# Convolution and two MLPs on one core: a new order of the first steps, and the low part of two chunks taken by one subtraction

## The chip, the cores and the metric

One core of a Trainium2 chip runs the whole program as one launch. The metric is device time in microseconds (us), the median of several executions of the same program.

## The reference

Each of 4 sequences of 4096 tokens with 192 channels goes through a causal convolution of 7 taps whose weights are a softmax per head (8 heads of 24 channels). The result, 16384 tokens by 192, goes through two MLPs with 2048 hidden units:

```python
w = softmax(weight)                                    # 8 heads x 7 taps
x = einsum('hk,bskhg->bshg', w, windows_of(x_padded))  # causal convolution
h = x @ w_in1;  x = (h - tanh(h)) @ w_out1             # first MLP
h = maximum(x @ w_in2, 0);  out = (h * h) @ w_out2     # second MLP
```

The inputs are float64 in memory, x apart. The kernel takes them as 64-bit words and makes two single-precision numbers of each weight, a high and a low part, so that products run as sums of high times high, high times low and low times high.

## The kernel before, in words

The tokens are cut into 32 blocks of 512. The hidden units are cut into 8 pairs of chunks, a chunk being 128 units. A **step** is one unit `(m, b, p)`: MLP m, block b, pair p. There are 512 of them, and `units` holds their order. The first two blocks of an MLP run interleaved, block 0 ahead of block 1 by `SKEW` pairs (`two_blocks`), so that each pair of weights, once ready, is used by two blocks; afterwards blocks run one by one (`one_block`), the first MLP a block ahead of the second.

In a step TensorE makes the products of the first layer for a pair (`products_1`, 18 matmuls, into two PSUM banks `ph`) and mixes them with the products of the second layer of the units two and three steps earlier (`products_2`, 20 matmuls, into the accumulators `pA` and `pB`; `LAG = 2`). All run on 64 of the 128 rows, two side by side. There are four `ph` banks, so step i+2 can't write before the banks of step i have been read.

The other engines of a step: ScalarE makes tanh of a chunk (L405), VectorE h minus tanh (L406); ScalarE copies the result, rounded, into `gh` (L417); VectorE subtracts `gh` from it and writes the low part `gl` (L419). `act` and `split` hold this, and the loop at the end of the kernel issues, per step: first part of the products, `split` of the second chunk of the step before, then matmuls, `act` of the first chunk, matmuls, `act` of the second chunk, `split` of the first. In the second MLP ScalarE makes Relu (L408) and Square (L412), save that in block 1 VectorE multiplies for every second chunk (L410).

VectorE and ScalarE have two more tasks in the first steps. Each pair of weights is **decoded** from 64-bit words once (`decode_ops`: L124, L129, L130, L134, L138 for the bits, L150, L155 and L160 for high and low parts). The **convolution** of a block is seven taps on VectorE (`tap`, L230, L233) per half of the channels (A: 128 channels of one block, B: 64 channels of two blocks), after a transposition (L265, L270). Only the first ones are made by TensorE, by matmuls with diagonal matrices (`pe_conv`, L254; the matrices by ScalarE, L248). `split_ops` makes the high and low part of a block's convolution, `z` (L297, L298, L302, L303), and SyncE copies half of it to the other 64 rows (L289).

All is issued in an order written out by hand (`tc.manual_schedule`): `prologue` for what comes ahead of step 0, and `side`, a list for every half step, into which `spread` lays the decodes, transpositions, taps and results. `due` says at which step a pair of weights is to be ready; its decode is spread over the two and a half steps ahead. Each engine runs its instructions in the order issued.

Of the kernel before, what the change touches and what calls it, by code (L numbers as in the profile page):

```python
# [10 lines left out]
F32 = mybir.dt.float32  # L11
F32R = mybir.dt.float32r
# [3 lines left out]
ALU = mybir.AluOpType  # L16
# [14 lines left out]
def conv_mlp_mlp_kernel(ctx: ExitStack, tc: tile.TileContext, x, weight, w_in1, w_out1, w_in2, w_out2, out):  # L31
# [13 lines left out]
    nc = tc.nc  # L45
    B, S, D = x.shape
# [19 lines left out]
    cv = ctx.enter_context(tc.tile_pool(name="cv", bufs=2))  # L66
    zp = ctx.enter_context(tc.tile_pool(name="zp", bufs=2))
    yp = ctx.enter_context(tc.tile_pool(name="yp", bufs=3))
    work = ctx.enter_context(tc.tile_pool(name="work", bufs=3))
    op = ctx.enter_context(tc.tile_pool(name="op", bufs=1))  # L70
    ps_h = ctx.enter_context(tc.tile_pool(name="ps_h", bufs=4, space=PSUM))
    ps_a = ctx.enter_context(tc.tile_pool(name="ps_a", bufs=2, space=PSUM))
# [137 lines left out]

    def load_a(b, q=None):
        if b == 1:
            t = work.tile([P, T], F32, name="t").rearrange("p (a c) -> p a c", c=32)
        else:
            t = cv.tile([P, TH, 32], F32, name="xa", bufs=1)
        xs["A", b] = t
        for j in range(4):
            (q or nc.sync).dma_start(out=t[32 * j : 32 * j + 32], in_=x_of(b)[j])
# [21 lines left out]

    diag = {}

    def make_diag(p):
        t = diag.setdefault("all", yp.tile([P, 4 * T], F32, name="y") if p == "B" else None)
        for k in range(K):
            n = k + K * (p == "A")
            d = diag[p, k] = t[:, n * P : (n + 1) * P]
            nc.scalar.mul(d, ident, taps[:, "AB".index(p), k : k + 1])  # L248

    def pe_conv(p, b):  # L250

        a = acc[p, b] = ps_h.tile([P, T], F32, name="ph")
        for k in range(K):
            nc.tensor.matmul(a, diag[p, k], xT[p, b][:, k : k + T], start=k == 0, stop=k == K - 1)  # L254

    def halo(dst, b, src):
        if b % BPB == 0:
# [80 lines left out]
    def products_2(m, b, p, i):  # L338

        if (m, b) not in acc_t:  # L340
            acc_t[m, b] = [ps_a.tile([P, T], F32, name=n) for n in ("pA", "pB")]
        pA, pB = acc_t[m, b]
        r = slice(0, P) if i is None else half(i)
        to_a, to_b = [], []
        for c in range(2):
            gh, gl = (t[r] for t in g_t[m, b, 2 * p + c])
# [53 lines left out]

    def act(m, b, f):
        ph = h_t[m, b, f // 2][f % 2]
        t = t_t[m, b, f] = work.tile([P, T], F32, name="t")
        if m == 0:
            nc.scalar.activation(t, ph, AF.Tanh)  # L405
            nc.vector.tensor_tensor(t, ph, t, op=ALU.subtract)  # L406
        else:
            nc.scalar.activation(t, ph, AF.Relu)  # L408
            if b == 1 and f % 2:
                nc.vector.tensor_tensor(t, t, ph, op=ALU.mult)  # L410
            else:
                nc.scalar.activation(t, t, AF.Square)  # L412

    def split(m, b, f):
        t = t_t.pop((m, b, f))
        gh = work.tile([P, T], F32R, name="gh", bufs=6)
        nc.scalar.copy(gh, t)  # L417
        gl = work.tile([P, T], F32R, name="gl", bufs=6)
        nc.vector.tensor_tensor(gl, t, gh.bitcast(F32), op=ALU.subtract)  # L419
        g_t[m, b, f] = gh, gl  # L420

    def finish_ops(m, b):
        pA, pB = acc_t.pop((m, b))
# [27 lines left out]
        ]  # L451


    SKEW = 4

    def two_blocks(m):

        order = [(m, 0, p) for p in range(SKEW)]
        for p in range(NP):
            order.append((m, 1, p))  # L460
            if p + SKEW < NP:
                order.append((m, 0, p + SKEW))
        return order

    def one_block(m, b):
        return [(m, b, p) for p in range(NP)]

    units = two_blocks(0) + one_block(0, 2) + two_blocks(1)
    for b in range(3, NBLK + 1):
        if b < NBLK:  # L470
            units += one_block(0, b)
# [18 lines left out]
    pairs = [(m, p) for m in range(2) for p in range(NP)]  # L490

    due = [at[0, 0, p] for p in range(NP)]
    due += [min(at[1, 0, p], 2 * NP + 1 + 9 * p // 4) for p in range(NP)]

    def prologue():
        nc.sync.dma_start(out=wt, in_=weight)
        load_b(0)
        load_a(0)
        load_w(0, 0, "i")
        load_a(1)  # L500
        load_w(0, 0, "o")
        load_w(0, 1)
# [8 lines left out]
        w0 = decode_ops(0, 0, parts=((0, CI), (CI, CW)))  # L511
        z0 = split_ops(0)
        make_diag("B")
        pe_conv("B", 0)
        head_a(0)
        make_diag("A")
        tap("A", 0, 0)
        tap("A", 0, 1)
        tap("A", 0, 2)
        head_a(1)  # L520
        pe_conv("A", 1)
        w0[0]()
# [90 lines left out]
```

## Time and profile before

| | us |
|---|---|
| median of 3 runs | 2321.87 (2321.36 to 2329.53) |
| profiled execution, its own time | 2329.7 |
| its span | 2327.9 |
| TensorE busy | 2309.2 (99%) |
| ScalarE busy | 1619.3 (70%) |
| VectorE busy | 1467.7 (63%) |
| mean granted TensorE clock | 0.996 |

Matmuls are pipelined in the profile, so a busy TensorE is not one at its pace: the number of matmuls in a stretch says more. Rows give the start of an instruction in us from the span's start, or its busy time; where VectorE's instructions follow each other without a wait, the next one starts a little before the one ahead ends, so that the distance of two starts is what an instruction takes of the queue.

### The profile page before, as it was taken

The page shows a single profiled execution, that of the slowest core. Times are in us where ns is not written, and L with a number is a line of the kernel's source. Part 1 is how long each engine was busy: PE and PEld are TensorE (multiplying, and loading weights), DVE is VectorE, ACT ScalarE, POOL GpSimd, SP SyncE. Part 2 cuts the span into 40 slices and gives each one's busy share as a digit, 9 for nine tenths or more (in the row PEclk, how much of TensorE's full clock was granted, in tenths as well). Part 3 has the DMA queues.
Part 4 walks back from the last instruction along what each step waited for, and adds up shares of the span by engine and source line. Part 5 has one row for each costly group of instructions (what it writes and reads, how often), then busy time and mean ns, then how long its engine had stood idle before and what let it go on. Part 6 is the DMA issues. An engine that isn't in the chain of part 4 may idle for free.

```text
span 2327.9 us, 50435 instructions
## 1 busy us (share of the span) xinstructions
PE 2309.2 (99%) x19500; PEld 1892.5 (81%) x19500; DVE 1467.7 (63%) x2299; ACT 1619.3 (70%) x2866; POOL 1.4 (0%) x15
## 2 busy tenths in 40 slices
PE   9999999999999999999999999999999999999999
PEld 6767888888888888888988888888888888888887
DVE  8986666656666555666557665566665666665553
ACT  5577766777666777667777667776677776677766
POOL 0000000000000000000000000000000000000000
PEclk8999999999999999999999999999999999999999
DMA  5230101101111101111001011010111011110000
GB/s 127 68 83 17 26 13 26 22 14 23 22 17 22 26 10 22 17 22 26 15 17 26 13 26 22 11 26 13 26 22 20 16 22 17 22 22 11 16 13 15
DMA packets 216864, 57.78 MB, mean 25 GB/s; under 512 B 204336, under 2 KB 210480, under 8 KB 216624
## 3 DMA queue, kind: packets, MB, share of 16 engines
q1 hardware_dynamic: 216624, 54.56, 11.6%
q8 instruction: 154, 2.52, 0.5%
q14 instruction: 86, 0.70, 0.1%
HBM read 25.17 MB, written 12.58 MB: 16 GB/s over the span
## 4 chain that ended last, share of the span: by engine, by line
PE 95%; DVE 2%; ACT 1%; issue 1%; DMA 0%; SPq 0%; POOL 0%; DVEq 0%; ACTq 0%; POOLq 0%
PE ph L359 38%; PE pA L359 33%; PE pB L359 22%; PE ph L254 1%; DVE t L406 0%; DVE da L138 0%; ACT gh L417 0%; DVE da L134 0%; PE ph L239 0%; DVE gl L419 0%; ACT t L405 0%; ACT da L124 0%; DVE da L129 0%; DVE wIl L155 0%; ACT t L408 0%
## 5 line engine op out<-in xcount | busy, mean ns | idle before, releaser
L359 PE MATMUL pA<-gh,wO 64*128 64x512 f32 x4088 | 1279.3, 392 | 0.0
L419 DVE TENSOR_TENSOR gl<-t,gh 128x512 fp32r<-128x512 f32 x1024 | 683.4, 688 | 623.2 <-ACT gh L417 589.9
L359 PE MATMUL ph<-z,wIh 64*128 64x512 f32 x3072 | 1011.0, 394 | 9.8 <-DVE t L406 7.4
L359 PE MATMUL ph<-y,wIh 64*128 64x512 f32 x3072 | 1003.2, 391 | 1.9 <-DVE t L410 1.9
L359 PEld LDWEIGHTS pA<-gh,wO 64*128 64x128 f32 x4088 | 753.9, 185 | 86.3 <-ACT gh L417 0.8
L359 PE MATMUL pB<-gl,wO 64*128 64x512 f32 x2044 | 804.4, 394 | 0.0
L359 PE MATMUL pB<-gh,wO 64*128 64x512 f32 x2044 | 801.7, 392 | 0.0
L359 PE MATMUL pA<-gl,wO 64*128 64x512 f32 x2044 | 800.8, 392 | 0.0
L417 ACT CAST gh<-t 128x512 fp32r<-128x512 f32 x1024 | 604.7, 613 | 99.1 <-DVE t L406 94.8
L359 PEld LDWEIGHTS ph<-z,wIh 64*128 64x128 f32 x3072 | 569.0, 185 | 75.3 <-DVE t L406 10.6
L359 PEld LDWEIGHTS ph<-y,wIh 64*128 64x128 f32 x3072 | 566.2, 184 | 60.5 <-DVE t L410 2.7
L359 PE MATMUL ph<-z,wIl 64*128 64x512 f32 x1536 | 604.7, 394 | 0.4 <-DVE wIl L155 0.3
L359 PE MATMUL ph<-y,wIl 64*128 64x512 f32 x1536 | 601.4, 392 | 0.0
L405 ACT ACTIVATE t<-ph 128x512 f32<-128x512 f32 x512 | 305.7, 598 | 364.2 <-PE ph L359 265.0
L406 DVE TENSOR_TENSOR t<-ph,t 128x512 f32<-128x512 f32 x512 | 351.9, 687 | 204.6 <-ACT t L405 203.7
L359 PEld LDWEIGHTS pA<-gl,wO 64*128 64x128 f32 x2044 | 376.8, 184 | 49.3 <-DVE gl L419 0.4
L359 PEld LDWEIGHTS pB<-gh,wO 64*128 64x128 f32 x2044 | 376.8, 184 | 48.0
L359 PEld LDWEIGHTS pB<-gl,wO 64*128 64x128 f32 x2044 | 376.4, 184 | 46.1
L408 ACT ACTIVATE t<-ph 128x512 f32<-128x512 f32 x512 | 305.1, 596 | 153.3 <-PE ph L359 130.4
L412 ACT ACTIVATE t<-t 128x512 f32<-128x512 f32 x504 | 318.8, 633 | 16.0
L359 PEld LDWEIGHTS ph<-z,wIl 64*128 64x128 f32 x1536 | 284.6, 185 | 28.4 <-DVE wIl L155 1.5
L359 PEld LDWEIGHTS ph<-y,wIl 64*128 64x128 f32 x1536 | 282.8, 184 | 27.5
(71 smaller groups left out, 712.0 us busy)
## 6 DMA issues: line engine op xcount, KB each, us to landing
z<-z SPq DMA_DIRECT2D x32, 256.0 KB
y<-y SPq DMA_DIRECT2D x32, 256.0 KB
out<-ua SPq DMA_DIRECT2D x128, 64.0 KB
xa<-in_x SPq DMA_DIRECT2D x124, 64.0 KB
st<-in_moe_w_out SPq DMA_DIRECT2D x16, 384.0 KB
xb<-in_x SPq DMA_DIRECT2D x64, 64.0 KB
st<-in_moe_w_in SPq DMA_DIRECT2D x16, 256.0 KB
out<-tu SPq DMA_DIRECT2D x64, 64.0 KB
```

The costliest lines, as they stand in the source:

```text
L254: nc.tensor.matmul(a, diag[p, k], xT[p, b][:, k : k + T], start=k == 0, stop=k == K - 1)
L359: ins = nc.tensor.matmul(o, w, r, start=start, stop=stop).ins
L405: nc.scalar.activation(t, ph, AF.Tanh)
L406: nc.vector.tensor_tensor(t, ph, t, op=ALU.subtract)
L408: nc.scalar.activation(t, ph, AF.Relu)
L412: nc.scalar.activation(t, t, AF.Square)
L417: nc.scalar.copy(gh, t)
L419: nc.vector.tensor_tensor(gl, t, gh.bitcast(F32), op=ALU.subtract)
```

## The change

Four things. First, the low part `gl` of both chunks of a pair is made by one subtraction over 1024 columns, after the second chunk's `gh`; the tiles `t`, `gh` and `gl` hold a pair. Second, in the prologue VectorE makes five of the taps of block 0's half A and TensorE the last two, whose sum VectorE adds (L258 of the changed kernel); the weights of pair 1 are decoded before step 0's results; block 1's convolution on TensorE follows step 0; loads of weights stand ahead of that of block 1; `pe_conv` writes to the accumulators' banks. Third, the interleaved blocks stand three pairs apart in place of four. Fourth, the pairs of the second MLP are due later, one every 2.5 steps from step 18 in place of every 2.25 from step 17, and block 3's convolution starts at step 30 in place of 17.

```diff
     def split(m, b, f):
-        t = t_t.pop((m, b, f))
-        gh = work.tile([P, T], F32R, name="gh", bufs=6)
-        nc.scalar.copy(gh, t)
-        gl = work.tile([P, T], F32R, name="gl", bufs=6)
-        nc.vector.tensor_tensor(gl, t, gh.bitcast(F32), op=ALU.subtract)
-        g_t[m, b, f] = gh, gl
+        p = f // 2
+        if f % 2 == 0:
+            g_t[m, b, p] = [work.tile([P, 2, T], F32R, name=n, bufs=3) for n in ("gh", "gl")]
+        gh, gl = g_t[m, b, p]
+        nc.scalar.copy(gh[:, f % 2], t_t[m, b, p][:, f % 2])
+        if f % 2:
+            nc.vector.tensor_tensor(gl, t_t.pop((m, b, p)), gh.bitcast(F32), op=ALU.subtract)
...
-    def pe_conv(p, b):
-        a = acc[p, b] = ps_h.tile([P, T], F32, name="ph")
-        for k in range(K):
-            nc.tensor.matmul(a, diag[p, k], xT[p, b][:, k : k + T], start=k == 0, stop=k == K - 1)
+    def pe_conv(p, b, first=0):
+        a = ps_a.tile([P, T], F32, name="p" + p)
+        for k in range(first, K):
+            nc.tensor.matmul(a, diag[p, k], xT[p, b][:, k : k + T], start=k == first, stop=k == K - 1)
+        if first:
+            nc.vector.tensor_tensor(acc[p, b], a, acc[p, b], op=ALU.add)
+        else:
+            acc[p, b] = a
...
-    SKEW = 4
+    SKEW = 3
...
-    due += [min(at[1, 0, p], 2 * NP + 1 + 9 * p // 4) for p in range(NP)]
+    due += [min(at[1, 0, p], 2 * NP + 2 + (5 * p + 1) // 2) for p in range(NP)]
...
         make_diag("B")
         pe_conv("B", 0)
         head_a(0)
-        make_diag("A")
-        tap("A", 0, 0)
-        tap("A", 0, 1)
-        tap("A", 0, 2)
-        head_a(1)
-        pe_conv("A", 1)
-        w0[0]()
-        for o in w0[1:4]:
+        make_diag("A", range(own, K))
+        for k in range(own):
+            tap("A", 0, k)
+        for o in w0[0:5]:
             o()
+        make_diag("A", range(own))
+        w0[6]()
+        w0[5]()
+        for o in w0[7:10]:
+            o()
+        pe_conv("A", 0, own)
         z0[0]()
...
         z0[1]()
         z0[2]()
+        for o in w0[10:]:
             o()
+        head_a(1)
+        w1[0]()
+        for o in w1[1:]:
+            o()
...
-    after = {}
-    spread(split_ops(1), 1, 4)
+    after = {0: [lambda: pe_conv("A", 1)]}
+    spread(split_ops(1), 3, 6)
...
-        a = {2: 4 * SKEW, 3: 4 * NP + 2}.get(b, s - 4 * NP)
+        a = {2: 4 * SKEW, 3: 2 * at[1, 0, 4]}.get(b, s - 4 * NP)
```

The built order shows three places. The first is VectorE's queue from the decode of pair 1 (`da` 128x768) to the low part of step 0; `t` is h minus tanh of a chunk. Before:

```order
L129 TENSOR_SCALAR da<-da 128x768
L130 TENSOR_SCALAR da<-da 128x768
L134 SCALAR_TENSOR_TENSOR da<-st,da 128x768
L138 SCALAR_TENSOR_TENSOR da<-st,da 128x768
L406 TENSOR_TENSOR t<-ph,t 128x512
L155 TENSOR_TENSOR wIl_83<-da,wIh_82 128x384
L160 TENSOR_TENSOR wO_84<-da,wO_84 128x2x128
L160 TENSOR_TENSOR wO_84<-da,wO_84 128x2x64
L406 TENSOR_TENSOR t<-ph,t 128x512
L419 TENSOR_TENSOR gl<-t,gh 128x512 x2
```

And in the change, from the transposition of block 1:

```order
L271 STREAM_TRANSPOSE xTa<-t 128x512
L129 TENSOR_SCALAR da<-da 128x768
L130 TENSOR_SCALAR da<-da 128x768
L134 SCALAR_TENSOR_TENSOR da<-st,da 128x768
L138 SCALAR_TENSOR_TENSOR da<-st,da 128x768
L155 TENSOR_TENSOR wIl_83<-da,wIh_82 128x384
L160 TENSOR_TENSOR wO_84<-da,wO_84 128x2x128
L160 TENSOR_TENSOR wO_84<-da,wO_84 128x2x64
L414 TENSOR_TENSOR t<-ph,t 128x512
L129 TENSOR_SCALAR da<-da 128x768
L130 TENSOR_SCALAR da<-da 128x768
L414 TENSOR_TENSOR t<-ph,t 128x512
```

The three instructions that end a decode (L155 and two of L160) have moved ahead of step 0's first subtraction, and the transposition of block 1 stands right ahead of the decode.

The second place is VectorE's queue in two of the interleaved steps, where the weights of the first MLP are still being decoded. Before:

```order
L406 TENSOR_TENSOR t<-ph,t 128x512
L419 TENSOR_TENSOR gl<-t,gh 128x512 x2
L134 SCALAR_TENSOR_TENSOR da<-st,da 128x768
L138 SCALAR_TENSOR_TENSOR da<-st,da 128x768
L406 TENSOR_TENSOR t<-ph,t 128x512
L155 TENSOR_TENSOR wIl_83<-da,wIh_82 128x384
L406 TENSOR_TENSOR t<-ph,t 128x512
L419 TENSOR_TENSOR gl<-t,gh 128x512 x2
```

In the change:

```order
L414 TENSOR_TENSOR t<-ph,t 128x512
L430 TENSOR_TENSOR gl<-t,gh 128x1024
L134 SCALAR_TENSOR_TENSOR da<-st,da 128x768
L138 SCALAR_TENSOR_TENSOR da<-st,da 128x768
L414 TENSOR_TENSOR t<-ph,t 128x512
L155 TENSOR_TENSOR wIl_83<-da,wIh_82 128x384
L414 TENSOR_TENSOR t<-ph,t 128x512
L430 TENSOR_TENSOR gl<-t,gh 128x1024
```

Between the second chunk's `t` and the subtraction that needs that chunk's `gh` there stood the first chunk's subtraction; now nothing does.

The third place is VectorE's queue in steps 21 and 22, the last but one of the first MLP there. Before, with a tap of block 3 (`accA`) and the fourth decode of the second MLP's weights:

```order
L134 SCALAR_TENSOR_TENSOR da<-st,da 128x768
L138 SCALAR_TENSOR_TENSOR da<-st,da 128x768
L233 SCALAR_TENSOR_TENSOR accA<-xTa,taps,accA 128x512
L406 TENSOR_TENSOR t<-ph,t 128x512
L155 TENSOR_TENSOR wIl_86<-da,wIh_85 128x384
L406 TENSOR_TENSOR t<-ph,t 128x512
L419 TENSOR_TENSOR gl<-t,gh 128x512 x2
L160 TENSOR_TENSOR wO_87<-da,wO_87 128x2x128
L160 TENSOR_TENSOR wO_87<-da,wO_87 128x2x64
L406 TENSOR_TENSOR t<-ph,t 128x512 x2
L419 TENSOR_TENSOR gl<-t,gh 128x512 x2
```

In the change, with the third decode:

```order
L134 SCALAR_TENSOR_TENSOR da<-st,da 128x768
L138 SCALAR_TENSOR_TENSOR da<-st,da 128x768
L414 TENSOR_TENSOR t<-ph,t 128x512
L155 TENSOR_TENSOR wIl_86<-da,wIh_85 128x384
L414 TENSOR_TENSOR t<-ph,t 128x512
L430 TENSOR_TENSOR gl<-t,gh 128x1024
L160 TENSOR_TENSOR wO_87<-da,wO_87 128x2x128
L160 TENSOR_TENSOR wO_87<-da,wO_87 128x2x64
L414 TENSOR_TENSOR t<-ph,t 128x512 x2
L430 TENSOR_TENSOR gl<-t,gh 128x1024
```

The tap is gone from here, and one decode fewer has been made by this point.

## Rows read from the trace of the kernel before

**Rows 1.** The page: share of the chain that ended last, by engine.

```profile
PE 95%; DVE 2%; ACT 1%; issue 1%; DMA 0%; SPq 0%; POOL 0%; DVEq 0%; ACTq 0%; POOLq 0%
```

**Rows 2.** Windows: us, busy (instructions) of each engine, granted clock, DMA share, GB/s.

```profile
23.00:50.00 27.00, 24.98 (x120) 18.24 (x121) 25.35 (x43) 14.89 (x28) 0.00 (x0) 0.75 0.52 138
50.00:100.00 50.00, 48.06 (x397) 39.40 (x396) 47.92 (x81) 28.40 (x54) 0.00 (x0) 0.97 0.32 80
100.00:150.00 50.00, 43.81 (x356) 32.65 (x354) 46.05 (x78) 32.14 (x60) 0.00 (x0) 1.00 0.32 85
150.00:200.00 50.00, 48.14 (x408) 37.70 (x406) 38.41 (x64) 41.78 (x76) 0.00 (x0) 1.00 0.13 38
200.00:300.00 100.00, 100.00 (x860) 80.27 (x860) 63.30 (x99) 71.31 (x128) 0.00 (x0) 1.00 0.12 22
```

**Rows 3.** Waits from 23 us on: us in total, times, longest.

```profile
PE ph L359 <- DVE t L406: 7.4, 9, 1.7
...
DVE t L406 <- ACT t L405: 3.8, 5, 1.6
```

**Rows 4.** Timeline of VectorE, two interleaved steps: start, duration, instruction, count, idle before.

```profile
56.10 0.95 DVE L134 SCALAR_TENSOR_TENSOR da<-st,da 128x768 uint32<-128x768 uint32 x1
...
57.96 0.68 DVE L406 TENSOR_TENSOR t<-ph,t 128x512 f32<-128x512 f32 x1
58.63 0.56 DVE L155 TENSOR_TENSOR wIl<-da,wIh 128x384 fp32r<-128x384 f32 x1
59.12 0.69 DVE L406 TENSOR_TENSOR t<-ph,t 128x512 f32<-128x512 f32 x1
59.73 1.47 DVE L419 TENSOR_TENSOR gl<-t,gh 128x512 fp32r<-128x512 f32 x2
61.11 0.62 DVE L160 TENSOR_TENSOR wO<-da,wO 128x256 fp32r<-128x256 f32 x2
61.65 0.68 DVE L406 TENSOR_TENSOR t<-ph,t 128x512 f32<-128x512 f32 x1
62.25 0.55 DVE L129 TENSOR_SCALAR da<-da 128x768 f32<-128x768 f32 x1
...
63.31 0.68 DVE L406 TENSOR_TENSOR t<-ph,t 128x512 f32<-128x512 f32 x1
```

**Rows 5.** Timeline of ScalarE, the same steps: the copy of the second chunk.

```profile
59.85 0.62 ACT L417 CAST gh<-t 128x512 fp32r<-128x512 f32 x1 [0.25 <-DVE t L406]
```

**Rows 6.** Timeline of VectorE: step 0's first subtraction, and the two of step 22.

```profile
26.44 0.69 DVE L406 TENSOR_TENSOR t<-ph,t 128x512 f32<-128x512 f32 x1
...
147.54 1.28 DVE L406 TENSOR_TENSOR t<-ph,t 128x512 f32<-128x512 f32 x2
```

**Rows 7.** Timeline of the prologue, all engines.

```profile
7.72 4.20 ACT L248 ACTIVATE y<-ua,taps 128x128 f32<-128x128 f32 x14
...
12.92 0.71 DVE L265 STREAM_TRANSPOSE xTa<-t 128x512 f32<-128x512 f32 x1 [2.69 <-DMA t<-in_x]
...
14.30 0.56 DVE L134 SCALAR_TENSOR_TENSOR da<-st,da 128x384 uint32<-128x384 uint32 x1
...
15.37 3.11 DVE L233 SCALAR_TENSOR_TENSOR accA<-xTa,taps,accA 128x512 f32<-128x512 f32 x4
...
16.17 6.17 PE L254 MATMUL ph<-xTa,y 128*128 128x512 f32 x14
```

**Rows 8.** Timeline of the second MLP's interleaved blocks, a step of block 1.

```profile
176.72 0.51 ACT L150 CAST wIh<-da 128x384 fp32r<-128x384 f32 x1 [1.54 <-DVE da L138]
...
178.34 0.68 DVE L410 TENSOR_TENSOR t<-t,ph 128x512 f32<-128x512 f32 x1
...
179.07 0.49 PE L359 MATMUL ph<-y,wIh 64*128 64x512 f32 x1 [1.26 <-DVE t L410]
```

**Rows 9.** Timeline of the last pair.

```profile
2317.50 1.29 DVE L419 TENSOR_TENSOR gl<-t,gh 128x512 fp32r<-128x512 f32 x2 [3.14 <-ACT gh L417]
...
2320.54 0.40 PE L359 MATMUL pA<-gl,wO 128*128 128x512 f32 x1
```

More of the change, by code (lines that the diff above doesn't have):

```diff
@@ L68, in conv_mlp_mlp_kernel @@
     yp = ctx.enter_context(tc.tile_pool(name="yp", bufs=3))
-    work = ctx.enter_context(tc.tile_pool(name="work", bufs=3))
+    work = ctx.enter_context(tc.tile_pool(name="work", bufs=2))
     op = ctx.enter_context(tc.tile_pool(name="op", bufs=1))
@@ L212, in load_a @@
         if b == 1:
-            t = work.tile([P, T], F32, name="t").rearrange("p (a c) -> p a c", c=32)
+            t = work.tile([P, 2, T], F32, name="t")[:, 0, :].rearrange("p (a c) -> p a c", c=32)
         else:
@@ L241, in conv_mlp_mlp_kernel, with make_diag @@
     diag = {}
-    def make_diag(p):
-        t = diag.setdefault("all", yp.tile([P, 4 * T], F32, name="y") if p == "B" else None)
-        for k in range(K):
+    def make_diag(p, ks=range(K)):
+        if not diag:
+            diag["all"] = yp.tile([P, 4 * T], F32, name="y")
+        t = diag["all"]
+        for k in ks:
             n = k + K * (p == "A")
@@ L248, in make_diag @@
             nc.scalar.mul(d, ident, taps[:, "AB".index(p), k : k + 1])
-    def pe_conv(p, b):
-        a = acc[p, b] = ps_h.tile([P, T], F32, name="ph")
-        for k in range(K):
-            nc.tensor.matmul(a, diag[p, k], xT[p, b][:, k : k + T], start=k == 0, stop=k == K - 1)
+    def pe_conv(p, b, first=0):
[6 more added lines that the diff above has]
+            acc[p, b] = a
     def halo(dst, b, src):
@@ L345, in products_2 @@
         for c in range(2):
-            gh, gl = (t[r] for t in g_t[m, b, 2 * p + c])
+            gh, gl = (t[r, c] for t in g_t[m, b, p])
             w = W[m]["O"][r, p, c]
@@ L402, in act @@
         ph = h_t[m, b, f // 2][f % 2]
-        t = t_t[m, b, f] = work.tile([P, T], F32, name="t")
+        if f % 2 == 0:
+            t_t[m, b, f // 2] = work.tile([P, 2, T], F32, name="t")
+        t = t_t[m, b, f // 2][:, f % 2]
         if m == 0:
@@ L414, in split @@
     def split(m, b, f):
-        t = t_t.pop((m, b, f))
-        gh = work.tile([P, T], F32R, name="gh", bufs=6)
-        nc.scalar.copy(gh, t)
-        gl = work.tile([P, T], F32R, name="gl", bufs=6)
-        nc.vector.tensor_tensor(gl, t, gh.bitcast(F32), op=ALU.subtract)
-        g_t[m, b, f] = gh, gl
+        p = f // 2
+        if f % 2 == 0:
+            g_t[m, b, p] = [work.tile([P, 2, T], F32R, name=n, bufs=3) for n in ("gh", "gl")]
[3 more added lines that the diff above has]
+            nc.vector.tensor_tensor(gl, t_t.pop((m, b, p)), gh.bitcast(F32), op=ALU.subtract)
     def finish_ops(m, b):
@@ L451, in finish_ops, with two_blocks @@
         ]
-    SKEW = 4
-    def two_blocks(m):
-        order = [(m, 0, p) for p in range(SKEW)]
+    SKEW = 3
+    def two_blocks(m, behind):
+        order = [(m, 0, p) for p in range(behind)]
         for p in range(NP):
             order.append((m, 1, p))
-            if p + SKEW < NP:
-                order.append((m, 0, p + SKEW))
+            if p + behind < NP:
+                order.append((m, 0, p + behind))
         return order
@@ L466, in one_block @@
         return [(m, b, p) for p in range(NP)]
-    units = two_blocks(0) + one_block(0, 2) + two_blocks(1)
+    units = two_blocks(0, SKEW) + one_block(0, 2) + two_blocks(1, 3)
     for b in range(3, NBLK + 1):
@@ L498, in prologue @@
         load_a(0)
-        load_w(0, 0, "i")
+        load_w(0, 0)
+        load_w(0, 1)
         load_a(1)
-        load_w(0, 0, "o")
-        load_w(0, 1)
         warm = wpool.tile([P, 1], F32, name="warm")
@@ L511, in prologue @@
         w0 = decode_ops(0, 0, parts=((0, CI), (CI, CW)))
+        w1 = decode_ops(0, 1)
         z0 = split_ops(0)
+        own = 5
         make_diag("B")
@@ L515, in prologue @@
         head_a(0)
-        make_diag("A")
-        tap("A", 0, 0)
-        tap("A", 0, 1)
-        tap("A", 0, 2)
-        head_a(1)
-        pe_conv("A", 1)
-        w0[0]()
-        for o in w0[1:4]:
-            o()
-        w0[4]()
-        for k in range(3, K):
-            tap("A", 0, k)
+        make_diag("A", range(own, K))
+        for k in range(own):
+            tap("A", 0, k)
+        for o in w0[0:5]:
+            o()
+        make_diag("A", range(own))
         w0[6]()
+        w0[5]()
+        for o in w0[7:10]:
+            o()
+        pe_conv("A", 0, own)
         z0[0]()
-        w0[5]()
         z0[1]()
         z0[2]()
-        for o in w0[7:]:
+        for o in w0[10:]:
             o()
-    after = {}
-    spread(split_ops(1), 1, 4)
-    for n in range(1, len(pairs)):
+        head_a(1)
[4 more added lines that the diff above has]
+    spread(split_ops(1), 3, 6)
+    side[0].append(lambda: load_w(0, 2))
+    for n in range(2, len(pairs)):
         ops = decode_ops(*pairs[n])
@@ L543, in conv_mlp_mlp_kernel @@
         d = 2 * due[n]
-        spread(ops, *((d - 2, d) if n < SKEW else (d - 5, d - 1)))
+        spread(ops, *((1, 4) if n == 2 else (d - 5, d - 1)))
     side[2 * SKEW] += [lambda: load_a(2), lambda: load_b(2)]
```

## The prediction

> **What bounds the kernel now.** The chain of waits is 95% TensorE [rows 1], so the time is TensorE's work plus what it loses. Where it loses is read from the windows by counting matmuls. From 200 us on 860 run in 100 us, 8.6 per us, and a step of 38 takes 38/8.6 = 4.42 us [rows 2]. Against that pace the stretch from 23 to 50 us lacks 232 - 120 = 112 matmuls, or 13.0 us; 50 to 100 lacks 33, or 3.8 us; 100 to 150 lacks 74, or 8.6 us; 150 to 200 lacks 22, or 2.6 us [rows 2]. After that nothing is lost. So this change has about 28 us and the head to win, and no more.
>
> Next comes what TensorE waits for. The largest releaser is L406, h minus tanh, which sets a `ph` bank free [rows 3]. VectorE is busy 25.4 of 27, 47.9 of 50 and 46.1 of 50 us up to 150 us [rows 2] and waits for ScalarE in L406 only 3.8 us [rows 3]. **Up to the end of the first MLP's first three blocks (steps 0 to 23) the kernel runs at the pace of VectorE's queue**, and TensorE follows it by two steps, the depth of the four banks. From 150 to 200 us VectorE has 38.4 and ScalarE 41.8 of 50 us [rows 2], and they wait for each other. I therefore cost the change as time of VectorE's queue from step 0 to step 22, add what becomes of the second MLP's two blocks, and take the rest as hidden.
>
> **One subtraction for two chunks.** Today the second chunk's L406 starts at 59.12. Its copy `gh` on ScalarE can start only when that is done and runs from 59.85 to 60.47 [rows 5]. VectorE meanwhile makes the first chunk's `gl`, starting at 59.73. The pair of subtractions ends at 61.20 [rows 4], so with 0.69 for the last it starts at 60.51, just behind the copy, and the next instruction starts at 61.11. From L406 to there the queue spends 1.99 us, of which it idles 0.1.
>
> In the change nothing stands between L406 and the subtraction, which needs the second copy. It can't start before the same 1.39 us have gone by (60.51 - 59.12), and then has 1024 columns. No such instruction is in the trace. From 384 to 768 columns L134 grows from 0.56 to 0.95 [rows 7, 4], so 0.26 per 256, and 1024 columns take 1.21 us; the next instruction starts about 0.08 earlier, as behind the pairs (61.20 to 61.11). So 1.39 + 1.13 = 2.52 us in place of 1.99: **0.53 us more per step**, with about 0.7 us of idling in it. Bounds: if the wait cost nothing, 0.60 + 1.13 = 1.73, or 0.26 less; if two 512-column subtractions' full time were needed behind the wait, 1.39 + 1.38 = 2.77, or 0.78 more. I take 0.53, since the wait follows from an in-order queue and the two rows beside it. Steps 0 to 21 lie ahead of step 22's first subtraction: 22 x 0.53 = **+11.7 us**.
>
> The Trainium skill (Perfetto Trace Analysis, section Optimizing Scalar/DVE Operations) says that grouping into larger operations can improve throughput where the engine is saturated. The trace agrees that it is saturated and that an instruction has a fixed part; by that rule alone the term would be 22 x -0.26 = -5.7 us in place of +11.7, which is the first rival below.
>
> **Fewer decodes before step 22.** A decode takes of the queue: L129 and L130 62.25 to 63.31, L134 and L138 56.10 to 57.96, L155 58.63 to 59.12, the two L160 61.11 to 61.65 [rows 4], in sum 1.06 + 1.86 + 0.49 + 0.54 = 3.95 us. With due steps 17, 19, 21, 23 four pairs of the second MLP were made by step 22, now with 18, 21, 23 three: **-4.0 us**. The end of pair 1's decode (L155 and two L160, 0.49 + 0.54) now stands ahead of step 0's first subtraction: **-1.0 us** from here on, and paid in the head. Block 3's transposition and two of its taps went from this stretch to step 30: three instructions of at most 0.78 [rows 7], taken at 0.6 each as they overlap: **-1.8 us** (bounds -1.4 and -2.3). The four terms give 11.7 - 4.0 - 1.0 - 1.8 = +4.9 us.
>
> **The head.** Step 0's first subtraction starts at 26.44 now [rows 6]. Off: the wait for block 1's load, 2.69 [rows 7], as the transposition comes eight or more us later (the load is issued behind five transfers of weights but is not needed until then); two of seven taps, 2 x 0.78 [rows 7], less the added sum, at about 0.65. On: two waits of VectorE for ScalarE, one for the copy of pair 0's weights (about 0.55) and one for the other half's bits behind five diagonal matrices (5 x 4.20/14 = 1.5 [rows 7]); the 1.0 above; and about 0.6, since ScalarE makes step 0's tanh behind the last copy of pair 1's weights. Sum: -2.7 - 0.9 + 2.1 + 1.0 + 0.6 = +0.1. The first subtraction stays at 26.5, between 25 and 28. TensorE's own order there (block 1's seven taps, 6.17 us [rows 7], behind step 0, and two taps more, 2/7 of that, ahead of it) is free: it waits for VectorE on both sides. If it were not, those two taps cost 1.8. In steps 1 and 2 I see one new wait: ScalarE's tanh of step 1 stands behind the copy of pair 2's weights, which waits for VectorE; about 1.1, against 0.5 of the same kind that goes: +0.6. Block 1's copy between halves on SyncE comes a step closer to its use; VectorE has work queued meanwhile, so 0, at worst the 2.7 that a late landing cost in row 12.92 [rows 7].
>
> So step 22's first subtraction moves from 147.54 [rows 6] to 147.54 + 4.9 + 0.1 + 0.6 = 153.1, and TensorE, which follows it, comes to the second MLP **about 5 us later** (3 to 7).
>
> **The second MLP's two blocks.** Here TensorE waits where a chunk of block 1 is multiplied on VectorE, L410: at 178.34 it stands behind a decode, the copy to `wIh` waits 1.54 for L138, and TensorE waits 1.26 [rows 8]. Now each decode has 2.5 steps in place of 2.25, but four and a half fall here in place of three and a half, with eight instructions of block 3's convolution in place of five. The same waits then come in two or three steps of block 1. I take 3.1 lost in place of 2.6: **+0.5** (bounds -2.6, all gone, and +3, twice as much).
>
> **The rest.** In the one-block order, from 200 us on, TensorE loses nothing [rows 2], and VectorE is busy 63 of 100 us, which covers 0.53 per step of 4.42. At the end the last pair's low parts are needed at 2320.54 and done at 2318.8 [rows 9]; 0.5 later is still ahead: 0. The deeper or shallower tiles change no wait: a pair's `gl` is read off by the same step as before.
>
> Sum: 5 + 0.5 = +5.5 us. The profiled execution took 2329.7, 7.8 above the median, so 2335.2 by its own time and 2321.9 + 5.5 = **2327.4 us** by the median. About 0.5%, or 11.6 us, is what a measurement of this kernel can tell from no change; this is half of it.
>
> **The rivals.**
> - *Grouping pays.* If the wait for the second copy cost nothing, the first term is -5.7 and the stretch gives -5.7 - 4.0 - 1.0 - 1.8 + 0.7 = -11.8, about the 12.4 that TensorE loses from 50 to 150 us, so hardly any is left over. With +0.5 the time is 2310.6. For it: VectorE is the bound [rows 2], and work leaves it. Against it: the two rows of L406 and the copy, and an order in which the two neighbours depend on each other through ScalarE. It is the case that the Trainium skill's rule (Perfetto Trace Analysis, Optimizing Scalar/DVE Operations) would give. 0.12.
> - *The terms cancel.* The 3.8 us that VectorE idles for ScalarE today [rows 3] vanish, because it is later everywhere, and the second MLP's decodes, further apart, give back their 2.6 and the 0.5: 5.5 - 3.8 - 3.1 = -1.4, so 2320.5. For it: slower decodes were asked for just where TensorE waits. Against it: ScalarE is as full there as before. 0.25.
> - *The clock falls* (the slower side). From 23 to 50 us TensorE was granted 0.75 on the mean, from 50 to 100 us 0.97, from 100 us on 1.00 [rows 2]: at the lower of its levels (1.2 GHz) for 27 x 0.25 x 2 = 13.5 and 3 us, after pauses. The pauses grow now. One more stretch of 13.5 us costs up to 6.8 in matmuls, with VectorE's lead at most a step to cover it: 2327.4 + 6.8 = 2334.2, and 2340 with two. It decides if steps 5 to 12, where block 2's convolution and the decodes meet, pause longer than those after 100 us, which lost 8.6 us in 50 at the full clock. 0.11.
>
> **How the numbers follow.** The forecast has 0.52; its own range, from the bounds of the queue (2 each way), the second MLP and the spread of the runs shown, is 2321 to 2333. The range takes in the cancelling case and most of the clock's, and leaves out most of the first rival: 2313 to 2335. Faster by over 0.5% (under 2310.3) takes two thirds of the first rival, 0.08, slower (over 2333.5) most of the clock case and the forecast's edge, 0.10, and within 0.5% 0.82.
>
> **What would show it.** In the profile after, a 1024-column subtraction of about 1.21 us stands in place of L419, with some 0.7 us of idle before it for `gh` in each step up to 150 us. The windows from 50 to 150 us lack more matmuls than the 107 of today. The page's VectorE busy time falls, since 512 x (1.38 - 1.21) = 87 us go. Step 0's first subtraction is near 26.5, step 22's near 153. The forecast is wrong if that idle is missing, if 50 to 150 us lacks fewer matmuls than before, or if the granted clock there is lower.

## The result, and the profile after

The change made the kernel slower: 2341.13 us median of 9 runs (2336.10 to 2347.01) against 2326.18 (2321.36 to 2330.15), a ratio of 1.0066 with a 95% interval from 1.0050 to 1.0083, or some 15 us. The prediction named 2327.4 and a range up to 2335. Of the 13.7 us between the two times 4.3 are the kernel before, whose median was 2321.87 in the three runs known then and is 2326.18 in nine; the change itself costs some 15 us where 5.5 were forecast. The profiled execution took 2341.13, its span is 2339.3.

The windows of the kernel after, with the columns of [rows 2]:

```profile
23.00:50.00 27.00, 23.27 (x84) 13.59 (x84) 17.48 (x27) 10.90 (x20) 0.00 (x0) 0.82 0.37 98
50.00:100.00 50.00, 44.44 (x350) 35.10 (x348) 41.58 (x63) 25.82 (x49) 0.00 (x0) 0.97 0.33 81
100.00:150.00 50.00, 45.09 (x362) 36.31 (x360) 42.03 (x61) 30.62 (x56) 0.00 (x0) 0.97 0.22 62
150.00:200.00 50.00, 45.65 (x370) 36.04 (x369) 36.84 (x53) 37.16 (x68) 0.00 (x0) 0.97 0.27 73
200.00:300.00 100.00, 100.00 (x864) 83.04 (x862) 71.25 (x93) 73.44 (x132) 0.00 (x0) 1.00 0.13 24
```

TensorE makes 36 matmuls fewer from 23 to 50 us, 41 fewer in the next 100 us and 38 fewer from 150 to 200. VectorE, which was 25.4 of 27 us busy at the start, is at 17.5; from 50 to 150 us it is at 83.6 of 100 where it had 94. It waits more, and TensorE waits for it.

Counted by steps (18, 18, 28 and then 38 matmuls, against 4.42 us for a full step), step 4 starts at 54.5 us in place of 47.7, so 6.7 later. Steps 4 to 23 lose 17.7 us in place of 13.1, and steps 24 to 39 lose 6.4 in place of 3.0. That is 14.7 us by step 40; the rest of the program runs 3.3 faster in this execution (the last section says at what pace).

Where it waits, by the waits view: the first two lines of VectorE from 23 to 150 us, then TensorE from 100 to 230 us.

```profile
DVE gl L430 <- ACT gh L428: 13.7, 20, 0.7
DVE t L414 <- ACT t L413: 7.3, 6, 4.1
...
PE pA L365 <- ACT gh L428: 3.4, 1, 3.4
PE pA L365 <- DVE y L444: 2.8, 1, 2.8
PE pA L365 <- DVE gl L430: 2.6, 6, 1.0
PE ph L365 <- DVE t L414: 0.3, 1, 0.3
```

The first line is new and is the one subtraction's wait for the second copy, 0.69 us each time. The second was 3.8 us [rows 3], and 4.1 of its 7.3 are one wait in the head. TensorE's waits for a `ph` bank, the largest before (5.5 us from 100 to 230 us), are nearly gone there; in their place it waits for the accumulator `pA` and for low parts.

VectorE's queue in a step, by the timeline (the answer to [rows 4]):

```profile
55.82 0.68 DVE L414 TENSOR_TENSOR t<-ph,t 128x512 f32<-128x512 f32 x1
57.19 1.23 DVE L430 TENSOR_TENSOR gl<-t,gh 128x1024 fp32r<-128x1024 f32 x1 [0.69 <-ACT gh L428]
58.33 0.95 DVE L134 SCALAR_TENSOR_TENSOR da<-st,da 128x768 uint32<-128x768 uint32 x1
```

From L414 to the next instruction it is 2.51 us, of which 0.69 idle; the prediction had 2.52 and about 0.7, against 1.99 before.

The head, TensorE's timeline first, VectorE's behind it (L256 is the convolution on TensorE), then two windows with the columns of [rows 2]:

```profile
19.86 0.79 PE L365 MATMUL ph<-z,wIh 64*128 64x512 f32 x1 [4.31 <-ACT z L304]
27.03 8.87 PE L256 MATMUL pA<-xTa,y 128*128 128x512 f32 x14
...
46.80 0.50 PE L365 MATMUL ph<-z,wIh 64*128 64x512 f32 x1 [1.47 <-DVE z L309]
...
49.08 0.58 PE L365 MATMUL ph<-z,wIh 64*128 64x512 f32 x1 [1.78 <-DMA z<-z]
...
26.30 0.69 DVE L414 TENSOR_TENSOR t<-ph,t 128x512 f32<-128x512 f32 x1
29.59 0.56 DVE L129 TENSOR_SCALAR da<-da 128x768 f32<-128x768 f32 x1 [2.60 <-ACT da L124]
...
39.21 0.69 DVE L414 TENSOR_TENSOR t<-ph,t 128x512 f32<-128x512 f32 x1 [4.10 <-ACT t L413]
...
158.92 1.28 DVE L414 TENSOR_TENSOR t<-ph,t 128x512 f32<-128x512 f32 x2
```

```profile
18.70:32.20 13.50, 12.34 (x24) 7.20 (x25) 9.40 (x18) 5.89 (x11) 0.00 (x0) 0.50 0.48 137
49.40:52.70 3.30, 3.30 (x18) 2.57 (x16) 2.62 (x5) 1.79 (x4) 0.00 (x0) 0.50 0.82 124
```

Step 0's first subtraction is at 26.30, as forecast (26.5); step 22's is at 158.92, where 153.1 was forecast. For step 0 lasts from 19.86 to 27.03, and block 1's convolution behind it takes 8.87 us where it took 6.17 [rows 7]: the granted clock is 0.50, the lower of its levels, from 18.7 to 32.2 us, over step 0 and the first 5 us of the convolution. Step 1 so starts near 35.8, and VectorE stands still 4.10 us for step 1's tanh, after 2.60 for the bits of pair 2, whose load had not landed. Then, in step 3, the first of block 1, TensorE waits 1.47 us for the low part of block 1's convolution (L309) and 1.78 us for SyncE's copy of it to the other rows, and the granted clock is 0.50 again behind these waits.

### The profile page after: what moved, and what is told of

It is laid out like the page before. It is cut to its first block, busy times and chain, and to the rows that moved or that the text cites. A ratio compares the mean times of both kernels' runs of the same rounds, so it can differ in the third digit from the quotient of the medians.

```text
span 2339.3 us, 48936 instructions
## 1 busy us (share of the span) xinstructions
PE 2309.7 (99%) x19504; PEld 2056.2 (88%) x19504; DVE 1418.7 (61%) x1786; ACT 1622.5 (69%) x2866; POOL 1.4 (0%) x15
## 3 DMA queue, kind: packets, MB, share of 16 engines
q8 instruction: 154, 2.52, 0.4%
## 4 chain that ended last, share of the span: by engine, by line
PE 93%; DVE 4%; ACT 2%; issue 1%; DMA 0%; SPq 0%; ACTq 0%; DVEq 0%
PE ph L365 43%; PE pA L365 30%; PE pB L365 19%; DVE t L414 1%; ACT gh L428 1%; DVE gl L430 0%; DVE da L134 0%; DVE da L138 0%; PE pA L256 0%; ACT da L124 0%; DMA st<-in_moe_w_in 0%; DVE da L129 0%; DVE accA L233 0%; ACT t L413 0%; DVE accB L233 0%
## 5 line engine op out<-in xcount | busy, mean ns | idle before, releaser
L430 DVE TENSOR_TENSOR gl<-t,gh 128x1024 fp32r<-128x1024 f32 x512 | 627.4, 1225 | 794.5 <-ACT gh L428 598.8
L365 PE MATMUL ph<-z,wIh 64*128 64x512 f32 x3072 | 987.9, 394 | 12.3 <-DVE t L414 4.6
L365 PE MATMUL ph<-y,wIh 64*128 64x512 f32 x3072 | 980.4, 392 | 0.0
L365 PEld LDWEIGHTS pA<-gh,wO 64*128 64x128 f32 x4088 | 737.9, 185 | 51.4 <-ACT gh L428 7.3
L365 PEld LDWEIGHTS ph<-z,wIh 64*128 64x128 f32 x3072 | 552.7, 185 | 53.6 <-ACT z L304 5.1
L365 PEld LDWEIGHTS ph<-y,wIh 64*128 64x128 f32 x3072 | 549.0, 185 | 33.8
L365 PEld LDWEIGHTS pB<-gh,wO 64*128 64x128 f32 x2044 | 377.7, 185 | 35.8
L414 DVE TENSOR_TENSOR t<-ph,t 128x512 f32<-128x512 f32 x512 | 346.3, 683 | 97.5 <-ACT t L413 93.8
```

The lines of the kernel that those rows point to most:

```text
L365: ins = nc.tensor.matmul(o, w, r, start=start, stop=stop).ins
L430: nc.vector.tensor_tensor(gl, t_t.pop((m, b, p)), gh.bitcast(F32), op=ALU.subtract)
```

## Experiments

Times are ratios to the kernel before, measured on the same chip, with 95% intervals (a ratio is not the quotient of the two medians); 0.1% is 2.3 us. What an edit of the changed kernel gives back is the difference of its ratio to 1.0066; where the two intervals overlap the time alone doesn't show it, and the start of a step in the trace is given with it. Three theories ran against each other: **Q**, the one subtraction makes VectorE's queue longer where that queue sets the pace; **H**, the head is lost by its new order or by the clock; **B**, three pairs apart bring the accumulators' banks too late.

**The two subtractions again.**

```diff
-        if f % 2:
-            nc.vector.tensor_tensor(gl, t_t.pop((m, b, p)), gh.bitcast(F32), op=ALU.subtract)
+        c = f % 2
+        nc.vector.tensor_tensor(gl[:, c], t_t[m, b, p][:, c], gh[:, c].bitcast(F32), op=ALU.subtract)
+        if c:
+            t_t.pop((m, b, p))
```

> The changed kernel with the low part again taken by two subtractions of 512 columns, all else kept. Theory Q (VectorE's queue: the one subtraction makes it wait about 0.7 us for the second copy in each step): the wait behind L414 goes, the distance from the second L414 to the instruction behind the subtractions falls from 2.50 to 1.98 us, and the 50 to 150 us windows lack some 5 us less of matmuls; time 2341 - 6 = 2335 (2331 to 2338), the rest of the loss staying. Theory B (the accumulators' banks are read too late with three pairs between the blocks) and theory H (the head at the low clock): within 2 us of 2341, since neither is touched.

Measured 2331.97 us, ratio 1.0023 (1.0008 to 1.0038): 10 us given back, two thirds of the loss. VectorE's timeline at the same place:

```profile
55.78 0.68 DVE L414 TENSOR_TENSOR t<-ph,t 128x512 f32<-128x512 f32 x1
56.38 1.47 DVE L430 TENSOR_TENSOR gl<-t,gh 128x512 fp32r<-128x512 f32 x2
57.77 0.95 DVE L134 SCALAR_TENSOR_TENSOR da<-st,da 128x768 uint32<-128x768 uint32 x1
```

The distance is 1.99 us again. By steps, 7.3 us come back in steps 4 to 23 and 4.1 in 24 to 39, together more than the 6 us that Q had put on the whole.

**The one subtraction alone**, on the kernel before.

```diff
...
-        gl = work.tile([P, T], F32R, name="gl", bufs=6)
-        nc.vector.tensor_tensor(gl, t, gh.bitcast(F32), op=ALU.subtract)
...
+        if f % 2:
+            nc.vector.tensor_tensor(gl, t_t.pop((m, b, p)), gh.bitcast(F32), op=ALU.subtract)
```

(and the tiles for a pair, which the run above has too.)

> The kernel before with the one subtraction over 1024 columns alone (and the pair tiles it needs). Theory Q: the four terms that are left of the queue are gone, the 22 x 0.53 = 11.7 us stay, and the second MLP's blocks lose some 3 us more: 2326 + 10 = 2336 (2333 to 2341), slower than before by about what its undoing gave back (9 to 10). If the loss came only of the one subtraction together with the three pairs or the new head: 2326 to 2330.

Measured 2342.89 us, ratio 1.0060 (1.0040 to 1.0081), about 14 us, a little more than Q had given. Alone it costs as much as the whole change. The windows:

```profile
23.00:50.00 27.00, 24.22 (x113) 19.01 (x113) 24.16 (x39) 14.25 (x25) 0.00 (x0) 0.68 0.51 136
50.00:100.00 50.00, 45.12 (x367) 36.95 (x366) 42.64 (x64) 26.79 (x51) 0.00 (x0) 1.00 0.32 81
100.00:150.00 50.00, 42.34 (x326) 28.97 (x324) 41.78 (x64) 29.20 (x54) 0.00 (x0) 1.00 0.26 67
150.00:200.00 50.00, 45.20 (x370) 33.60 (x368) 38.59 (x55) 35.96 (x66) 0.00 (x0) 1.00 0.22 56
```

From 50 to 150 us 60 matmuls fewer than before, 7.0 us, and 38 fewer in the next 50, 4.4 us, all of it at the full clock. The clock is no part of this. (It is lower from 23 to 50 us, 0.68 against 0.75, where 7 matmuls are missing.)

**The one subtraction behind other work.** Its place alone changes.

```diff
             for o in side[2 * i]:
                 o()
+            if i:
+                low(*before)
             run(10, 13)
...
```

(`low` is the subtraction, taken out of `split`; behind the loop it stands once more for the last pair.)

> The changed kernel with the one subtraction kept, but issued behind the half step's other work (decodes, taps, results), so that VectorE has something to do while ScalarE copies the second chunk. Theory Q: the 0.69 us of idling goes in all half steps that have such work, the queue of steps 0 to 23 is about as short as with two subtractions, 2341 - 9 = 2332 (2329 to 2335). Theory L (it is the lateness of the first chunk's low part that costs, not VectorE's idling): the low parts come later still, TensorE waits more for gl, and the time stays at 2339 to 2345.

Measured 2329.22 us, ratio 1.0017 (1.0007 to 1.0026): 11 us given back with the large subtraction kept. So it is the wait that costs, not the size. VectorE's timeline shows decode and transpositions where it idled:

```profile
64.53 0.68 DVE L414 TENSOR_TENSOR t<-ph,t 128x512 f32<-128x512 f32 x1
65.13 0.95 DVE L134 SCALAR_TENSOR_TENSOR da<-st,da 128x768 uint32<-128x768 uint32 x1
...
68.21 1.18 DVE L432 TENSOR_TENSOR gl<-t,gh 128x1024 fp32r<-128x1024 f32 x1
69.31 0.68 DVE L414 TENSOR_TENSOR t<-ph,t 128x512 f32<-128x512 f32 x1
```

The rival L (a late low part) isn't empty: by the waits view TensorE waits 6.7 us for `gl` up to 150 us here, against 2.4 in the changed kernel. It is the smaller of the two.

**The old head**: prologue, convolution on TensorE and first decodes as before, in the changed kernel.

```diff
-    after = {0: [lambda: pe_conv("A", 1)]}
-    spread(split_ops(1), 3, 6)
+    after = {}
+    spread(split_ops(1), 1, 4)
```

(and `prologue`, `make_diag` and `pe_conv` of the kernel before.)

> The changed kernel with the prologue, the convolution on TensorE and the decode order of the first steps as before, all else kept. Theory H: TensorE's pause of 4.3 us ahead of step 0 and the low clock behind it go, step 4 starts near 48 us in place of 54.5, time 2341 - 6 = 2335 (2332 to 2337). If VectorE's queue set the pace from the start (theory Q alone), the head would not count and the time stays within 2 us of 2341.

Measured 2335.98 us, ratio 1.0049 (1.0034 to 1.0064), 4 us back; step 4 starts at 48.8 us in place of 54.5. The two intervals overlap, but the trace and a second pair of runs say the same: with two subtractions the ratio is 1.0023 with the new head (above) and 1.0000 with the old one (the rest alone, below), 5 us. H holds, and TensorE's order in the head cost what the prediction had at nothing.

**Clock or order?** First 16 small matmuls in TensorE's pause:

```diff
         pe_conv("A", 0, own)
+        warm_pe(16)
```

> The changed kernel with 16 small matmuls of no use in TensorE's pause ahead of step 0. Theory H1 (the head is lost to the low clock): the granted clock from 18.6 to 32.3 us is the high one, step 0 takes 4.4 us in place of 7.2 and block 1's convolution 6.2 in place of 8.9, step 1 starts near 30.5 in place of 35.8, and the time falls by 3 to 5 to 2337 (2335 to 2339). Theory H2 (the head is lost to the order alone: the decode of pair 1, the late load of pair 2 and the convolution between steps 0 and 1 would hold it up at either clock): step 4 moves by less than 2 us and the time stays within 2 of 2341.

Measured 2341.33 us, ratio 1.0063 (1.0042 to 1.0084): no change, step 4 at 54.4. But the matmuls didn't do what they were for. TensorE's timeline and the windows:

```profile
15.11 3.73 PE L239 MATMUL ph<-ua 128*128 128x128 f32 x32
20.75 0.50 PE L365 MATMUL ph<-z,wIh 64*128 64x512 f32 x1 [1.91 <-ACT z L304]
27.79 8.21 PE L256 MATMUL pA<-xTa,y 128*128 128x512 f32 x14
```

```profile
10.00:20.00 10.00, 8.84 (x45) 5.77 (x43) 6.56 (x14) 3.56 (x9) 0.00 (x0) 1.00 0.45 117
20.00:30.00 10.00, 9.25 (x21) 5.88 (x22) 7.10 (x14) 3.74 (x8) 0.00 (x0) 0.57 0.58 169
```

A pause of 1.91 us was left, and the clock still fell behind it. What the head would take at the full clock this run doesn't tell.

Then the order, by the convolution behind step 1:

```diff
-    after = {0: [lambda: pe_conv("A", 1)]}
-    spread(split_ops(1), 3, 6)
+    after = {1: [lambda: pe_conv("A", 1)]}
+    spread(split_ops(1), 4, 6)
```

> The changed kernel with block 1's convolution on TensorE issued behind step 1 in place of step 0. Theory H2 (the order: the convolution, 8.9 us at the low clock, holds step 1 up, and VectorE waits 4.1 us for step 1's tanh): step 1 starts near 28 in place of 35.8, VectorE's 4.1 us of idling in front of step 1's first subtraction is under 1, and step 4 starts 2 to 4 us earlier; time 2341 - 3 = 2338 (2336 to 2340). Theory H1 (the low clock behind the pause sets it wherever the convolution stands): step 4 within 1 us of 54.5 and 2339 to 2343.

Measured 2332.72 us, ratio 1.0044 (1.0025 to 1.0063), 5 us back with overlapping intervals; the median lies under H2's range. The timelines of TensorE and VectorE:

```profile
33.28 8.76 PE L256 MATMUL pA<-xTa,y 128*128 128x512 f32 x14
...
30.27 0.56 DVE L129 TENSOR_SCALAR da<-da 128x768 f32<-128x768 f32 x1 [2.64 <-ACT da L124]
...
36.86 0.69 DVE L414 TENSOR_TENSOR t<-ph,t 128x512 f32<-128x512 f32 x1 [1.07 <-ACT t L413]
```

The convolution takes as long as in the changed kernel, the first 5 us of it again at the low clock, but step 1 starts at 26.6 and VectorE's wait is 1.07 in place of 4.10. TensorE's two waits for block 1's `z` in step 3 are gone. Step 4 starts at 50.7, 3.8 earlier. So of the 5.7 us between the two heads 3.8 go with the convolution's place, while the low clock up to step 4 lasts some 17 us in either (0.81 on the mean from 10 to 54.4 us in the changed kernel, 0.79 from 10 to 50.7 here). The wait for pair 2's load is left.

**Four pairs apart**, in the changed kernel:

```diff
-    SKEW = 3
+    SKEW = 4
...
-    units = two_blocks(0, SKEW) + one_block(0, 2) + two_blocks(1, 3)
+    units = two_blocks(0, SKEW) + one_block(0, 2) + two_blocks(1, 4)
```

> The changed kernel with the interleaved blocks four pairs apart again (and block 2's load and convolution from steps 4 and 8 as before), all else kept. Theory B: the waits of 3.4 us in step 18 and 2.8 us in step 29 on an accumulator go, and with them two stretches at the low clock; time 2341 - 8 = 2333 (2330 to 2336). Theory Q alone: a decode of the first MLP is due a step earlier, so VectorE has no less to do: 2341 to 2344.

Measured 2343.13 us (4 runs), ratio 1.0071 (1.0049 to 1.0093): nothing given back. **The results read earlier**, with three pairs kept:

```diff
-                lambda: nc.scalar.copy(tb, pB[DB:P]),
-                lambda: nc.vector.tensor_tensor(tb, pB[0:DB], tb, op=ALU.add),
-                lambda: nc.scalar.copy(zt[:, 0, 0], pA),
+                lambda: [nc.scalar.copy(tb, pB[DB:P]), nc.scalar.copy(zt[:, 0, 0], pA)],
+                lambda: [
+                    nc.vector.tensor_tensor(zt[:, 0, 1], pA, zt[:, 0, 0].bitcast(F32), op=ALU.subtract),
+                    nc.vector.tensor_tensor(tb, pB[0:DB], tb, op=ALU.add),
+                ],
...
-                lambda: nc.vector.tensor_tensor(zt[:, 0, 1], pA, zt[:, 0, 0].bitcast(F32), op=ALU.subtract),
```

> The changed kernel with a block's results of the first MLP read out of the accumulators two steps earlier (the same instructions, those that read PSUM first), three pairs apart kept. Theory B: as for the four pairs, the waits in steps 18 and 29 go, 2341 - 8 = 2333 (2331 to 2337). If the wait in step 18 was for the copy gh, which the profile names, and the one in step 29 is only VectorE's lateness: 2339 to 2342.

Measured 2338.66 us, ratio 1.0052 (1.0035 to 1.0068), 3 us back, which the intervals don't tell from nothing; in the trace step 40 starts 2.8 us earlier (234.8 against 237.6). It lies between the two theories. The waits view of TensorE from 100 to 230 us, four pairs first, then the earlier reading:

```profile
PE pA L365 <- DVE gl L430: 6.5, 16, 1.0
PE ph L365 <- DVE t L414: 1.7, 4, 0.7
```

```profile
PE pA L365 <- DVE gl L430: 4.8, 10, 1.1
PE ph L365 <- DVE t L414: 1.7, 4, 0.7
```

In both the two long waits on an accumulator are gone, so B named them rightly: the wait of 3.4 us in step 18, put down to the copy `gh`, was for L444 that frees `pA` (it ended at 133.4 us, and TensorE went on at 133.52; the copy named is of a later unit, which that step doesn't read). But most of the time comes back in later steps as waits for `gl`: steps 20 to 23 lose 4.1 and 4.0 us here, 0.9 in the changed kernel. With the large subtraction in place VectorE's queue stays too long, and the loss shows at another wait.

**The rest alone**: three pairs, later decodes and later convolution of block 3, with the old head and two subtractions.

> The kernel before with the blocks three pairs apart and the later decodes and convolution of block 3 alone (two subtractions and the old prologue). By theories Q and H together the two bad parts are out and what is left is the relief of VectorE's queue, 4 + 1.8 us in steps 0 to 23, less the waits on the accumulators in steps 18 and 29: 2326 - 2.5 = 2323.5 (2319 to 2327). Theory B (three pairs apart cost by themselves): slower than before, 2329 to 2334.

Measured 2325.97 us, ratio 1.0000 (0.9988 to 1.0011). The waits view of TensorE, 100 to 230 us:

```profile
PE pA L359 <- ACT gh L422: 2.4, 1, 2.4
PE pA L359 <- DVE y L440: 2.1, 1, 2.1
```

The relief of VectorE is there (steps 20 to 23 lose nothing, where the kernel before loses 4.2 us) and the accumulators take it back in steps 18 and 28.

**The rest, with the results read earlier.** Both edits above together.

> The kernel before with three pairs apart, later decodes and later convolution of block 3, and with the results of a block of the first MLP read out of the accumulators two steps earlier. Theory B (in that kernel the accumulators are what is left: it lost 4.2 us in steps 18 and 19 and 4.0 in 28 and 29): 2326 - 6 = 2320 (2316 to 2322), faster than before by 0.2 to 0.4%. Theory Q alone (VectorE's queue would only show the loss in a later step, as it did where four pairs were tried on the changed kernel): 2323 to 2327.

Measured 2315.51 us, ratio 0.9972 (0.9957 to 0.9986), faster than both kernels. The windows:

```profile
23.00:50.00 27.00, 24.96 (x129) 18.92 (x129) 24.88 (x43) 16.04 (x28) 0.00 (x0) 0.75 0.57 145
50.00:100.00 50.00, 46.50 (x391) 37.65 (x389) 48.06 (x81) 27.91 (x53) 0.00 (x0) 1.00 0.24 60
100.00:150.00 50.00, 47.68 (x398) 36.55 (x396) 45.66 (x76) 33.59 (x61) 0.00 (x0) 1.00 0.29 80
150.00:200.00 50.00, 49.53 (x424) 39.48 (x422) 39.54 (x66) 42.15 (x78) 0.00 (x0) 1.00 0.22 59
```

From 100 to 200 us 58 matmuls more than before [rows 2], 6.7 us. The waits view of TensorE from 23 to 230 us has no wait on an accumulator left; its longest line is

```profile
PE ph L359 <- DVE t L408: 7.0, 9, 1.8
```

Where the queue is short enough, B's waits are a cost of their own.

**The same with the one subtraction behind other work**, and **at four pairs**:

> The same with the one subtraction over 1024 columns issued behind the half step's other work. Theory Q: with the wait covered, the one subtraction takes 1.13 us of the queue in place of 1.37 for the two and their wait, so 0.24 a step, 5 us over steps 0 to 23, of which TensorE's own pace leaves some 2: 2318 (2314 to 2322), the fastest of all. Theory L (the first chunk's low part comes too late for TensorE): 2324 to 2330, slower than the kernel with two subtractions.

Measured 2318.19 us, ratio 0.9975 (0.9963 to 0.9987): as fast as with two subtractions by the ratio, not faster. The 0.24 us a step that it saves of the queue don't show. In the traces it is behind: step 40 starts at 219.7 us against 215.8, and from 23 to 150 us TensorE waits for low parts, which it doesn't with two subtractions. So theory L holds in part.

```profile
PE pA L359 <- DVE gl L426: 8.6, 10, 1.9
```

> The kernel before with the later decodes, the later convolution of block 3 and the earlier reading of the accumulators, at four pairs apart. Theory Q: steps 0 to 23 are relieved of a decode and three instructions, 4.0 + 1.8 us, without the three pairs' waits on the accumulators: 2326 - 5 = 2321 (2318 to 2324). If three pairs apart are what relieves the first steps: 2325 to 2328, and slower than the kernel with three pairs and the earlier reading.

Measured 2318.66 us, ratio 0.9980 (0.9966 to 0.9993). By the ratios three pairs and four pairs can't be told apart once the accumulators are read early; in the traces three pairs are 3.9 us ahead at step 40 (215.8 against 219.8).

## Why the prediction was wrong

**What bounds the kernel** was right. VectorE's queue sets the pace of steps 0 to 23: adding to it alone (the one subtraction) made the kernel 0.6% slower, and covering the wait gave that back.

**One subtraction for two chunks** was right in mechanism and size: 2.51 us measured where 2.52 was forecast, and 0.69 of idling. The rule of the Trainium skill (Perfetto Trace Analysis, section Optimizing Scalar/DVE Operations), that grouping can improve throughput on a saturated engine, was the first rival. This case goes against it as the change stands, since the group must wait for its last member; with that wait covered, the large subtraction was no faster than two. The term's price in time was 10 us in the changed kernel (the two subtractions again) and 14 alone, for 11.7 forecast; but in steps 4 to 23, where the forecast had it, 7.3 and 9.4, and most of the rest in steps 24 to 39 (4.1 and 3.1), where it had none.

**The sum of the stretch**, +4.9 us, held: steps 4 to 23 lost 17.7 us in place of 13.1, +4.6. On VectorE it is read best with the old head, from step 0's first subtraction to step 22's:

```profile
27.19 0.68 DVE L408 TENSOR_TENSOR t<-ph,t 128x512 f32<-128x512 f32 x1
...
153.42 1.28 DVE L408 TENSOR_TENSOR t<-ph,t 128x512 f32<-128x512 f32 x2
```

That is 126.2 us against 121.1 before [rows 6], +5.1, where the terms that apply there (all but pair 1's decode) give +5.9. That it came so near is in part luck, for both sides of the sum were too large: the one subtraction alone made this distance 10.0 us longer, not 11.7, and the rest alone made it 3.4 shorter, not 5.8; there TensorE's wait of 2.4 us on an accumulator, in step 18, lies in the same stretch.

**The head** is the step that failed: "TensorE's own order there (block 1's seven taps, 6.17 us [rows 7], behind step 0, and two taps more, 2/7 of that, ahead of it) is free: it waits for VectorE on both sides." It wasn't. At the lower clock step 0 took 7.2 us (4.1 before, at the full one) and the convolution 8.9, so that step 1 came 8.5 us later than before and VectorE waited 4.10 us for it. I had given step 0 no time of its own and read the convolution from a row at the full clock. Moving it behind step 1 gave 3.8 us of trace. Two more terms failed beside it. Block 1's copy between halves was put at "0, at worst the 2.7": TensorE waited 1.78 us for it, and 1.47 for the low part ahead of it. The load of pair 2 (2.60 us of VectorE) was missed. Altogether step 4 came 6.7 us later, where the forecast had +0.7.

**The second MLP's two blocks**, +0.5, measured +3.4. "The deeper or shallower tiles change no wait" looked at the pair tiles and left out the accumulators: with three pairs, block 1 of the second MLP asks for its accumulator in step 29, a step sooner, while L444 frees it in step 28, behind the longer queue. In steps 24 to 39 the two subtractions gave back 4.1 us, where I had VectorE's idling at nothing. In their trace TensorE's waits for `gl` from 150 to 230 us (1.5 us) are gone, the wait on the accumulator is 1.9 us in place of 2.8, and the granted clock stays at 1.00. So of the 8.6 us by which the 14.7 at step 40 exceed the forecast's three parts (0.7, 4.9 and 0.5) 6.0 are the head and 2.9 the second MLP's blocks.

**The rivals.** Grouping pays: no, not as the change stands. The terms cancel: no. (The rest alone comes out at 1.0000, but by other terms: the relief of the queue against the accumulators.) The clock falls, the slower side: the time came out there, but not so. Steps 5 to 12 have no new stretch at the low clock. Before there were one of 13.7 us and one of 3.4; now one as long, earlier, covers step 0 and a part of the convolution, and three short ones stand behind the waits of steps 3, 18 and 29; the one subtraction alone lost its 14 us with a granted clock of 1.00 from 50 to 200 us. Of the loss two parts stand by their undoing, the subtraction (10 us) and the head (4 to 5 us); together undone they leave nothing. What the low clock costs in the head stays open.

**The signs.** The 1024-column subtraction (1.23 us) and its idling came, and from 50 to 150 us 148 matmuls are lacking where it was 107. VectorE's busy time fell by 49 us (1467.7 to 1418.7), not 87. And the granted clock from 100 to 150 us is 0.97, where it was 1.00, which the prediction had named as a sign of being wrong.

## What to carry to other kernels

Before two operations are made one, look at what the later input waits for: a subtraction that stood between a producer and its consumer may have been the only cover of a trip to another engine, and in a saturated in-order queue that trip is paid each time. Issue the large one behind work that needs nothing, or leave it in two. And when an order brings a consumer of a bank forward, move the instruction that frees the bank as well; here that alone turned a change worth nothing into 0.3%.

## What was not expected

TensorE has two paces at the same granted clock. From 200 to 300 us the profiled execution of before made 860 matmuls [rows 2] and that of after 864, both at 1.00, with the same matmuls in the program. Over steps 40 to 500 the kernel before took 2039.1 us (4.433 a step), the changed one 2035.6 and the fastest 2031.0 (4.415 a step). The changed one lies between because it went from one pace to the other on its way:

```profile
500.00:1000.00 500.00, 500.00 (x4306) 415.19 (x4304) 300.30 (x370) 354.89 (x626) 0.20 (x2) 1.00 0.11 20
1500.00:2000.00 500.00, 500.00 (x4290) 476.54 (x4288) 299.90 (x369) 352.59 (x622) 0.20 (x2) 1.00 0.11 21
```

Within one kernel the runs fall into groups some 4 to 5 us apart (before: near 2321, 2326 and 2330). The pace would make such groups: the five profiled executions that took 2031.0 us for these steps are each in the lowest group of their kernel's runs, the five that took over 2039 among the highest. What sets the pace wasn't tested. It is why single runs of this kernel can't settle 5 us, and why the traces are compared at step 40.
